# Left-over tokens of two batches interleaved in their buffer, and the last four stores walked token by token

## The chip, the cores and the metric

The kernel runs on one core of one Trainium2 chip. The metric is the device time of one execution in microseconds (us). The core has five engines that work side by side, each in its own program order: TensorE (PE, matrix products; PEld is its weight load), VectorE (DVE), ScalarE (ACT), GpSimd (POOL) and SyncE (SP). In this kernel SP issues every transfer; the transfers themselves are carried out by 16 DMA engines, between device memory and the on-chip buffers.

## The reference

The reference is an attention with keys and values averaged over blocks of 8 tokens, and two feed-forward blocks behind it:

```python
# q, k, v: 8 batches, 8 heads, 576 tokens, 64 per head
k_p = k.reshape(B, H, Sp, 8, D).mean(axis=3)
v_p = v.reshape(B, H, Sp, 8, D).mean(axis=3)
attn = softmax(q @ k_p^T / sqrt(D))
x = (attn @ v_p), heads side by side          # 4608 tokens x 512
h = x @ w_in                                   # 512 -> 1024
solu = h * softmax(h)
x = layernorm(solu) * g_ln @ w_out             # 1024 -> 512
h = ((x @ w1) * (x @ w2)) @ w3                 # 1024 -> 1024
out = h @ w_out2                               # 1024 -> 512, 4608 rows
```

All of it is in 32-bit floating point. Row 576 b + s of the output belongs to token s of batch b.

## The kernel before

**Tiles.** The 4608 tokens are nine blocks of 512. Blocks 0 to 7 are the first 512 tokens of the eight batches. Each batch has 64 tokens left over (`TL = S - 512`), and the eight left-overs together are block 8 (`j == B`). Up to the end of the first feed-forward block the unit of work is 256 tokens (`U`): 18 units, two to a block.

**First part.** Attention and the first feed-forward block run as one program in time slots (`put`, `after`). The instructions of every engine stand in the order in which the slots give them out. For each batch `Group.av` multiplies the softmax weights with the values. The result lies transposed, with 128 features on the partitions and tokens along the row, one call for each of the `NP = 4` feature chunks `p`. Of a batch's second group 256 tokens go on at once (`split`, an ACT copy at L100 and a DVE subtraction at L101), and the 64 left-over tokens are copied by DVE at L564 into the buffer `X8`. There are two such tiles, `X8[0]` for batches 0 to 3 and `X8[1]` for batches 4 to 7, 128 x (4 chunks x 256 tokens). Those copies number 8 batches x 4 chunks = 32. When units 16 and 17 come, `Rows.split_x` reads one `X8` tile each as a whole, and `Rows.chunk` takes its 256 tokens in two runs of 128.

So a token keeps its column of `X8` through everything behind it. Columns 128 i to 128 i + 127 of `X8[h]` become the 128 partitions of the output tile t = 2 h + i of block 8, and those 128 tokens come from batches 2 t and 2 t + 1.

**Second part.** Behind a stretch that prepares weights, the second feed-forward block runs block by block, `j` from 0 to 8, with all five engines in program order. `ab` makes the products (lines 948 to 950), `out_fc` adds them up in four accumulators `acc` (lines 994 to 997), and behind the last of eight steps `finish` ends the accumulators one after the other. `evac` scales each into an `ot` tile, 128 x 512, on DVE for even t (L1003) and on ACT for odd t (L1005), and SP issues its store (L1010). The four stores of a block are 256 KB each. For blocks 0 to 7, one row of 512 numbers per partition goes to a row of the output of its own. For block 8 the output rows lie in two batches, 576 rows apart.

The program ends when SP, at L1083, has seen every transfer land and the engines have met one another there.

Of the kernel before, what the change touches and what calls it, by code (L numbers as in the profile page):

```python
# [18 lines left out]
def attention_moe_kernel(  # L19
# [25 lines left out]
    nc = tc.nc  # L45

    B, H, S, D = q.shape
# [9 lines left out]
    TL = S - 512  # L57
    NB = B + 1
    NU = 2 * NB
    U = 256  # L60
# [12 lines left out]
    def bank(name):  # L73
        return PS.tile([P, 512], F32, tag="ba", name=name, bufs=3)
# [24 lines left out]
    def split(hi, lo, src):  # L99
        nc.scalar.activation(hi, src, AF.Copy)  # L100
        nc.vector.tensor_tensor(lo, src, hi.bitcast(F32), ALU.subtract)  # L101
# [43 lines left out]
    X8 = [X8P.tile([P, NP, U], F32, tag=f"X8{i}", name=f"X8{i}") for i in range(2)]  # L145
# [265 lines left out]
    class Group:  # L411
# [125 lines left out]
        def av(self, i):  # L537
            w, bt = self.width, self.batch
            if i == 0:
                X[self.a] = [M.tile([P, NP, U], F32R, tag=t, name=f"{t}{self.a}") for t in ("xh", "xl")]  # L540
            x = X[self.a]
            for p in (2 * i, 2 * i + 1):
                if self.g or p % 2 == 0:
                    av_bank = bank(f"av{self.a}_{p}")
                av = av_bank if self.g else av_bank[:, p % 2 * U : p % 2 * U + U]
                pair = lambda t: t[:, 2 * p : 2 * p + 2].rearrange("p a d -> p (a d)")
                vhp = VBDh[:, p].rearrange("p a d -> p (a d)")
                vlp = VBDl[:, p].rearrange("p a d -> p (a d)")
                terms = [
                    (vhp, self.pth[:, p, 0:w]),  # L550
                    (vhp, self.ptl[:, p, 0:w]),
                    (vlp, self.pth[:, p, 0:w]),
                    (pair(bt.vlh), self.ptx[:, 0:w]),
                    (pair(VLL), self.ptx[:, 0:w]),
                ]
                for n, (l, r) in enumerate(terms):
                    nc.tensor.matmul(av[:, 0:w], l, r, start=(n == 0), stop=(n == 4))  # L557
                if self.g == 0 and p % 2:
                    ps = slice(p - 1, p + 1)
                    split(x[0][:, ps], x[1][:, ps], av_bank.rearrange("p (c n) -> p c n", c=2))  # L560
                elif self.g == 1:
                    split(x[0][:, p], x[1][:, p], av[:, 0:U])
                    c0 = TL * (bt.b % 4)
                    nc.vector.tensor_copy(X8[bt.b // 4][:, p, c0 : c0 + TL], av[:, U : U + TL])  # L564


    class Rows:
# [216 lines left out]
    with tc.manual_schedule(engines={mybir.EngineType.PE, mybir.EngineType.SP}):  # L784
        for s_ in range(min(events), SLOTS * (NU + 1) + 2):
# [3 lines left out]
            u, c = s_ // SLOTS, s_ % SLOTS  # L789
# [209 lines left out]
    def evac(j, t):  # L999
        ot = M2.tile([P, C], F32, tag="ot", name=f"ot{j}_{t}", bufs=4)  # L1000
        k = kap[:, 4 * j + t : 4 * j + t + 1]
        if t % 2 == 0:
            nc.vector.tensor_scalar(ot, accs[t], k, None, ALU.mult)  # L1003
        else:
            nc.scalar.activation(ot, accs[t], AF.Copy, scale=k)  # L1005
        if j == B:
            to = out.rearrange("(b s) c -> b s c", s=S)[2 * t : 2 * t + 2, 512:S, :]
        else:
            to = out[S * j : S * j + 512, :].rearrange("(p t) c -> p t c", t=4)[:, t]
        nc.sync.dma_start(to, ot)  # L1010
# [3 lines left out]
    def finish():  # L1014

        nonlocal accs
        j, fc, pp = pend
        if fc == 0:
            accs = [bank(f"acc{j}_{t}") for t in range(4)]
        if fc < FC - 1:  # L1020
            for t in range(4):
                out_fc(fc, pp, t, False)
            for t in range(4):
                out_fc(fc, pp, t, True)
        else:
            for t in range(4):
                out_fc(fc, pp, t, False)
                out_fc(fc, pp, t, True)
                evac(j, t)
# [58 lines left out]
```

## Time and profile before

| | |
|---|---|
| median of three runs | 1296.38 us (1295.6 to 1296.57) |
| span of the profiled execution, first to last instruction | 1294.6 us |
| median less that span | 1.78 us |
| PE busy, share of the span | 1233.1 us, 95% |
| DVE busy | 807.7 us, 62% |
| ACT busy | 524.4 us, 41% |
| POOL busy | 406.1 us, 31% |
| granted TensorE clock, mean | 0.987 |
| stores of the output | 36, of 256 KB each |

The profile gives a span for the execution that it recorded and no total time of its own; the last 1.78 us of the median are what lies around the span, and they are carried along unchanged below. "Busy" counts the time in which an engine executes instructions; a share is an average over the whole span and says nothing of a stretch in which only one thing is left to wait for.

### The profile page before, as it was taken

To read this page: it belongs to the slowest core of one execution; us is meant where nothing else is said; L and a number is where in the kernel's file an instruction comes from. 1 tells how busy PE (TensorE), PEld (TensorE's weight loads), DVE (VectorE), ACT (ScalarE), POOL (GpSimd) and SP (SyncE) were. 2 spreads that over 40 slices of the span, in tenths; PEclk is the share of its full clock that TensorE was granted. 3 is DMA by queue.
4 is the path that set the end of the run, shared out by engine and by line. 5 is a ranking of instruction groups with operands and counts; after the bars stand their busy time and mean duration, and the time that the engine had idled before them with its cause. 6 is when DMAs were issued, how large, how long until landed. Compare 5 with 4: busy or idle time off the path is not lost.

```text
span 1294.6 us, 21828 instructions
## 1 busy us (share of the span) xinstructions
PE 1233.1 (95%) x8278; PEld 1126.2 (87%) x8278; DVE 807.7 (62%) x1595; ACT 524.4 (41%) x1480; POOL 406.1 (31%) x497
## 2 busy tenths in 40 slices
PE   7879999999999999999999999999999999999992
PEld 5669889888999888998987999999999999999991
DVE  6878777787878787635476454645454545454541
ACT  5554656666666666644354121212121212121210
POOL 3332534343534352300000243333333342424210
PEclk9989999999999999999999999999999999999996
DMA  9554556453646463223142011101010101010100
GB/s 232 123 131 126 143 128 166 116 162 110 174 117 171 116 163 110 74 74 114 41 170 83 1 33 34 58 10 66 1 66 1 66 1 66 1 66 1 34 1 33
DMA packets 85698, 109.43 MB, mean 85 GB/s; under 512 B 43608, under 2 KB 43608, under 8 KB 85592
## 3 DMA queue, kind: packets, MB, share of 16 engines
q1 hardware_dynamic: 85592, 108.03, 29.3%
q8 instruction: 65, 1.06, 0.3%
q14 instruction: 41, 0.34, 0.1%
HBM read 78.65 MB, written 29.36 MB: 83 GB/s over the span
## 4 chain that ended last, share of the span: by engine, by line
PE 73%; DVE 10%; DMA 7%; ACT 4%; issue 3%; POOL 1%; SPq 1%; POOLq 0%; DVEq 0%; ACTq 0%
PE p L948 9%; PE p L950 9%; PE p L949 9%; PE h L588 8%; PE acc L994 5%; PE acc L997 5%; PE acc L996 5%; PE x L646 3%; PE x L647 3%; PE x L645 3%; DMA f<-in_moe_w_dram 3%; PE av L557 2%; DMA kv<-in_v_dram 2%; PE lt L631 2%; DVE cvb L180 2%
## 5 line engine op out<-in xcount | busy, mean ns | idle before, releaser
L968 POOL TENSOR_TENSOR a<-a,b 128x256 f32<-128x256 f32 x72 | 53.0, 736 | 477.3 <-DVE b L967 477.3
L952 ACT ACTIVATE p<-p 128x256 f32<-128x256 f32 x72 | 27.9, 387 | 397.3 <-PE p L950 365.3
L645 PE MATMUL x<-lnh,gwh 128*128 128x256 f32 x576 | 166.4, 289 | 0.0
L646 PE MATMUL x<-lnl,gwh 128*128 128x256 f32 x576 | 163.0, 283 | 1.7 <-DVE lnl L635 1.7
L647 PE MATMUL x<-lnh,gwl 128*128 128x256 f32 x576 | 162.8, 283 | 0.0
L189 POOL TENSOR_TENSOR cvb<-cvb,cvm 128x512 f32<-128x512 f32 x46 | 61.0, 1326 | 187.3 <-DVE cvm L182 181.6
L473 ACT ACTIVATE ea<-sc,mx 128x72 f32<-128x72 f32 x320 | 98.6, 333 | 39.6 <-DVE mx L470 39.6
L997 PE MATMUL acc<-wfl,ph 128*128 128x512 f32 x288 | 113.1, 393 | 0.0
L996 PE MATMUL acc<-wfh,ph 128*128 128x512 f32 x288 | 112.9, 392 | 0.0
L646 PEld LDWEIGHTS x<-lnl,gwh 128*128 128x128 f32 x576 | 110.1, 191 | 2.8 <-DVE lnl L635 1.9
L645 PEld LDWEIGHTS x<-lnh,gwh 128*128 128x128 f32 x576 | 109.9, 191 | 1.0 <-DVE lnl L635 0.2
L647 PEld LDWEIGHTS x<-lnh,gwl 128*128 128x128 f32 x576 | 110.0, 191 | 0.0
L967 DVE TENSOR_TENSOR b<-b,p 128x256 f32<-128x256 f32 x72 | 30.2, 420 | 123.0 <-PE p L950 123.0
L588 PE MATMUL h<-winh,xh 128*128 128x512 f32 x288 | 98.8, 424 | 0.0
L588 PE MATMUL h<-winl,xh 128*128 128x512 f32 x288 | 90.0, 394 | 0.0
L588 PE MATMUL h<-winh,xl 128*128 128x512 f32 x288 | 89.4, 392 | 0.0
L948 PE MATMUL p<-th,w1h 128*128 128x256 f32 x288 | 81.6, 283 | 1.1 <-ACT p L952 1.1
L994 PE MATMUL acc<-wfh,pl 128*128 128x512 f32 x288 | 82.4, 392 | 0.0
L949 PE MATMUL p<-th,w1h 128*128 128x256 f32 x288 | 81.5, 283 | 0.0
L950 PE MATMUL p<-th,w1l 128*128 128x256 f32 x288 | 81.5, 283 | 0.0
L635 DVE TENSOR_TENSOR lnl<-lt,lnh 128x512 fp32r<-128x512 f32 x72 | 49.2, 686 | 51.2 <-ACT lnh L634 50.8
L956 DVE TENSOR_TENSOR u<-p,p 128x256 f32<-128x256 f32 x72 | 30.4, 422 | 77.3 <-PE p L950 76.2
(201 smaller groups left out, 3728.1 us busy)
## 6 DMA issues: line engine op xcount, KB each, us to landing
f<-in_moe_w_dram SPq DMA_DIRECT2D x32, 512.0 KB, 6.0
x2d<-xo SPq DMA_DIRECT2D x36, 256.0 KB, 2.0
xq<-x2d SPq DMA_DIRECT2D x36, 256.0 KB, 2.8
out_dram<-ot SPq DMA_DIRECT2D x36, 256.0 KB, 2.7
kv<-in_k_dram SPq DMA_DIRECT2D x32, 256.0 KB, 3.7
q<-in_q_dram SPq DMA_DIRECT2D x32, 256.0 KB, 7.5
kv<-in_v_dram SPq DMA_DIRECT2D x32, 256.0 KB, 6.7
f<-in_moe_w_out_dram SPq DMA_DIRECT2D x16, 512.0 KB, 6.2
```

Of the source, the lines that this page charges most:

```text
L189: self.engine.tensor_tensor(self.f, self.f, self.m.bitcast(F32), ALU.add)
L473: nc.scalar.activation(e[0:n, x], half[a][:, h], AF.Exp, bias=mx[0:n, x : x + 1], scale=1.0, accum_out=sm[0:n, x : x + 1],)
L588: nc.tensor.matmul(self.ph[:, a], s_[:, c], w_[:, c, a * 512 : a * 512 + 512], start=first, stop=last)
L645: nc.tensor.matmul(o, gw[0][:, f, ws], self.th[:, f], start=(f == 0), stop=False)
L646: nc.tensor.matmul(o, gw[0][:, f, ws], self.tl[:, f], start=False, stop=False)
L647: nc.tensor.matmul(o, gw[1][:, f, ws], self.th[:, f], start=False, stop=(f == FC - 1))
L948: nc.tensor.matmul(o, wh[:, c, fsl], th[:, c], start=c == 0, stop=False)
L949: nc.tensor.matmul(o, wh[:, c, fsl], tl[:, c], start=False, stop=False)
L950: nc.tensor.matmul(o, wl[:, c, fsl], th[:, c], start=False, stop=c == 1)
L994: nc.tensor.matmul(accs[t], pl[:, ts], wh, start=False, stop=(fc == FC - 1))
L996: nc.tensor.matmul(accs[t], ph[:, ts], wh, start=(fc == 0), stop=False)
L997: nc.tensor.matmul(accs[t], ph[:, ts], wl, start=False, stop=False)
```

## The change

Two places are edited. The copy at L564 writes the 64 left-over tokens of a batch to every second column of a run of 128 columns, so that column 2 s + b holds token s of batch b of the pair, where before the two batches' tokens lay in two runs of 64. The view of the output at the last four stores follows: it names the 64 tokens first and the two batches second.

```diff
@@ -560,8 +560,8 @@
                 elif self.g == 1:
                     split(x[0][:, p], x[1][:, p], av[:, 0:U])
-                    c0 = TL * (bt.b % 4)
-                    nc.vector.tensor_copy(X8[bt.b // 4][:, p, c0 : c0 + TL], av[:, U : U + TL])
+                    left = X8[bt.b // 4][:, p].rearrange("p (g s b) -> p g b s", g=2, b=2)[:, bt.b % 4 // 2, bt.b % 2]
+                    nc.vector.tensor_copy(left, av[:, U : U + TL])
@@ -1004,7 +1004,7 @@
         if j == B:
-            to = out.rearrange("(b s) c -> b s c", s=S)[2 * t : 2 * t + 2, 512:S, :]
+            to = out.rearrange("(b s) c -> s b c", s=S)[512:S, 2 * t : 2 * t + 2, :]
         else:
             to = out[S * j : S * j + 512, :].rearrange("(p t) c -> p t c", t=4)[:, t]
         nc.sync.dma_start(to, ot)
```

The instructions of PE, DVE, ACT and POOL stand in the same order as before. On SP the last four stores differ, at the very end of its program; `ot_0` to `ot_3` are the four output tiles, and behind each stands the shape of the output's view, outermost first:

```order
 L1010 DMA out_dram<-ot_2_13222 128x512
 L1010 DMA out_dram<-ot_3_13228 128x512
-L1010 DMA out_dram<-ot_0_13790 2x64x512
-L1010 DMA out_dram<-ot_1_13796 2x64x512
-L1010 DMA out_dram<-ot_2_13802 2x64x512
-L1010 DMA out_dram<-ot_3_13808 2x64x512
+L1010 DMA out_dram<-ot_0_13790 64x2x512
+L1010 DMA out_dram<-ot_1_13796 64x2x512
+L1010 DMA out_dram<-ot_2_13802 64x2x512
+L1010 DMA out_dram<-ot_3_13808 64x2x512
 L1083 UNCONDITIONAL_BRANCH
```

Nothing has moved; the two outer sizes of the four stores have changed places. The two lines above them are stores of block 7, whose view is 128 rows.

## Rows read from the trace of the kernel before

**Rows 1.** The profile's page: span, busy time, and DMA packets by size.

```profile
span 1294.6 us, 21828 instructions
PE 1233.1 (95%) x8278; PEld 1126.2 (87%) x8278; DVE 807.7 (62%) x1595; ACT 524.4 (41%) x1480; POOL 406.1 (31%) x497
...
DMA packets 85698, 109.43 MB, mean 85 GB/s; under 512 B 43608, under 2 KB 43608, under 8 KB 85592
```

**Rows 2.** Busy time by stretch at the end; last columns clock, DMA share, GB/s.

```profile
1269.40:1270.50 1.10, 1.10 (x6) 0.69 (x4) 0.51 (x1) 0.60 (x1) 0.00 (x0) 1.00 0.03 7
1270.50:1274.00 3.50, 0.13 (x1) 0.00 (x0) 0.24 (x1) 0.69 (x1) 0.00 (x0) 1.00 0.12 26
1274.00:1293.00 19.00, 0.00 (x0) 0.00 (x0) 0.00 (x0) 0.00 (x0) 0.00 (x0) 0.52 0.13 50
1293.00:1293.50 0.50, 0.00 (x0) 0.00 (x0) 0.00 (x0) 0.00 (x0) 0.00 (x0) 0.50 0.03 12
1293.50:1294.60 1.10, 0.00 (x0) 0.00 (x0) 0.00 (x0) 0.00 (x0) 0.00 (x0) 0.50 0.00 0
```

**Rows 3.** Timeline of block 8's evictions and stores: start, us, engine, line.

```profile
1268.63 0.75 DVE L1003 TENSOR_SCALAR ot<-acc,kap 128x512 f32<-128x512 f32 x1 [0.75 <-PE acc L994]
...
1269.31 0.69 ACT L1005 ACTIVATE ot<-acc,kap 128x512 f32<-128x512 f32 x1 [2.15 <-PE acc L994]
...
1269.41 10.67 SPq L1010 DMA_DIRECT2D out_dram<-ot  x4
...
1270.67 0.69 ACT L1005 ACTIVATE ot<-acc,kap 128x512 f32<-128x512 f32 x1 [0.67 <-PE acc L994]
```

**Rows 4.** L1010, block 8's four stores: issue ns min/median/max, first and last start.

```profile
L1010 SPq DMA_DIRECT2D out_dram<-ot x4: 559/2390/5035, 1269.4 to 1275.0; - x4
```

**Rows 5.** Who waited for whom on SP, from 1265 us to the end.

```profile
SPq L1083 <- DMA out_dram<-ot: 13.5, 2, 8.4
SPq L1083 <- PEq L1083: 0.6, 2, 0.4
```

**Rows 6.** L1010, block 7's four stores, with time to landing.

```profile
L1010 SPq DMA_DIRECT2D out_dram<-ot x4: 332/335/338, 1209.9 to 1211.8; - x4
...
DMA to landing us min/median/max: 2.8/2.8/2.8
```

**Rows 7.** Timeline: block 7's last eviction.

```profile
1211.07 0.69 ACT L1005 ACTIVATE ot<-acc,kap 128x512 f32<-128x512 f32 x1 [0.68 <-PE acc L994]
```

**Rows 8.** Busy time by stretch around block 7's stores; last columns as in rows 2.

```profile
1208.00:1210.50 2.50, 2.50 (x12) 1.79 (x11) 1.94 (x5) 0.69 (x1) 0.00 (x0) 1.00 0.00 0
1210.50:1214.00 3.50, 3.50 (x30) 3.42 (x29) 1.49 (x3) 1.26 (x3) 1.43 (x2) 1.00 0.89 300
1214.00:1216.00 2.00, 2.00 (x19) 2.00 (x18) 1.46 (x4) 0.45 (x1) 0.00 (x0) 1.00 0.00 0
```

**Rows 9.** L300, the loads of keys (views 64 x 2 x 512): issue ns min/median/max.

```profile
L300 SPq DMA_DIRECT2D kv<-in_k_dram x32: 597/604/780, 1.3 to 453.4; - x32
```

**Rows 10.** Timeline of SP at the program's start, with two such loads.

```profile
0.74 0.45 SPq L95 DMA_DIRECT2D gT<-in_moe_g_ln_dram  x1
1.25 1.40 SPq L300 DMA_DIRECT2D kv<-in_k_dram  x2
2.69 0.72 SPq L308 DMA_DIRECT2D KL<-in_k_dram  x1
3.46 0.39 SPq L157 DMA_DIRECT2D f<-in_moe_w_in_dram  x1
```

**Rows 11.** Busy time by stretch there; last columns as in rows 2.

```profile
2.80:3.20 0.40, 0.00 (x0) 0.00 (x0) 0.03 (x1) 0.00 (x0) 0.40 (x2) 1.00 0.62 159
3.20:3.60 0.40, 0.00 (x0) 0.00 (x0) 0.40 (x2) 0.00 (x0) 0.40 (x2) 1.00 0.76 282
3.60:4.00 0.40, 0.00 (x0) 0.00 (x0) 0.30 (x3) 0.00 (x0) 0.40 (x2) 1.00 1.04 292
```

**Rows 12.** L1083, the program's end: SP's closing instructions from 1290 us on.

```profile
L1083 SPq EVENT_SEMAPHORE  x6: 17/28/28, 1293.6 to 1294.6; - x6
```

**Rows 13.** L564, the copies into X8, and who waited for them (us, times).

```profile
L564 DVE COPY X<-av x32: 212/215/217, 81.4 to 561.5; 128x64 f32<-128x64 f32 x32
...
  PE pt L518: 5.7, 6
  PE av L557: 0.4, 1
  PEld sc L452: 0.2, 1
```

**Rows 14.** Three other lines of DVE: ns min/median/max, starts, shapes.

```profile
L180 DVE SCALAR_TENSOR_TENSOR cvb<-f,cvb x56: 640/692/1670, 12.3 to 544.1; 128x512 int32<-128x512 int32 x56
L529 DVE TENSOR_TENSOR ptl<-pt,pth x40: 417/681/693, 32.9 to 549.4; 128x512 fp32r<-128x512 f32 x32, 128x256 fp32r<-128x256 f32 x8
L406 DVE TENSOR_TENSOR sl<-vl,sh x8: 220/1001/1059, 31.9 to 469.9; 64x64 f32<-64x64 f32 x8
```

## The prediction

> **What bounds the kernel now.** The page gives a span of 1294.6 us with PE busy for 95% of it [rows 1]. That share says that PE sets the time while there is work for PE. It does not say what sets the end, so I read the last stretch by itself, as a table of busy time. From 1274 us to the end no engine computes anything: PE, DVE, ACT and POOL are all at zero, and all that moves is data at 50 GB/s [rows 2]. The timeline gives the start of this tail. Block 8's four accumulators are scaled out one after the other; the last of these evictions, on ACT, starts at 1270.67 us and takes 0.69 us, so it ends at 1271.36 [rows 3]. From there to the end of the span are 1294.6 - 1271.36 = 23.2 us with nothing but the four output stores. The view of waits agrees: SP's closing wait is for these stores, 13.5 us in two waits, and there is no other of size [rows 5].
>
> Why is the tail long? The four stores hold 4 x 256 KB = 1.05 MB. Between 1274 and 1293 us the mean busy share of the 16 DMA engines is 0.13 [rows 2], and 0.13 x 16 = 2.1: two engines, at 50 / 2 = 25 GB/s each, carry everything. 1.05 MB at 50 GB/s is 21 us, which is the tail but for its ends. Two is also the outermost size of the store's view of the output, two batches.
>
> **The same stores elsewhere in this trace.** Block 7 ends in the same way: two DVE and two ACT evictions, four stores of 256 KB, but the view's outermost size is 128. Its last eviction starts at 1211.07 and ends at 1211.76 us [rows 7]. Data flows from 1210.5 to 1214.0 us at a DMA share of 0.89 and 300 GB/s, and the share is 0.00 behind 1214.0 [rows 8]; 3.5 us x 300 GB/s is again 1.05 MB. So these data stop at latest 1214.0 - 1211.76 = 2.24 us behind the last eviction. SP issues each store in 0.34 us [rows 6]; in block 8 an issue takes between 0.56 and 5.04 us [rows 4].
>
> **The change part by part.** *The stores.* The outermost size becomes 64. No store of this kind is in the trace, but loads of the keys have just these views, 64 x 2 x 512 on both sides, 256 KB each. Their issue takes 0.60 us [rows 9]. At the program's start two of them are issued at 1.25 us, ahead of a load of 128 KB at 2.69 us [rows 10], and from 3.2 to 4.0 us the DMA share is 0.76 to 1.04 at 282 to 292 GB/s [rows 11]. So an outermost size of 64 brings close to all 16 engines, and an issue costs 0.60 - 0.34 = 0.26 us more than block 7's.
>
> The Trainium skill (DMA: Bandwidth & Descriptors, section "Why a DMA increments its semaphore by 16 and not by 1") has a rule for this: a transfer runs on the largest number of engines, up to 16, that divides the outermost size of both its sides. By it 2 gives two engines, with which the share of 0.13 agrees, and 64 against the tile's 128 partitions gives 16; a store with 64 outermost is what no run here shows yet. It would leave the sum as it is and speaks against the narrow rivals below.
>
> The new tail is then, from the last eviction's end: 2.24 us until the data stop, as behind block 7; 0.26 us for the longer issue; and the program's own end. Of that end, the old tail shows the size: some data still move between 1293.0 and 1293.5 us, 12 GB/s x 0.5 us = 6 KB, which at 50 GB/s is 0.12 to some 0.3 us of flow as one or both engines finish, so the data stop near 1293.3, and 1.3 us later the span ends [rows 2]. Sum 2.24 + 0.26 + 1.3 = 3.8 us, against 23.2 us. The span becomes 1271.4 + 3.8 = 1275.2 us, 19.4 us less. The landing time of block 7's stores gives nearly the same by another way: 2.8 us from issue to landing [rows 6], 0.26 for the longer issue and the 1.0 us from SP's first closing instruction behind the data, at 1293.6 us, to the end [rows 12] make 4.1.
>
> Bounds for this term: without the longer issue, and with block 7's data stopping up to 0.3 us before its stretch's edge, 3.2 us. If the stores run at the lower rate of the loads, 282 for 300 GB/s, and both the issue's 0.26 us and a first piece of data late by as much again come on top, 2.24 + 0.25 + 0.52 + 1.3 = 4.3 us. What hides the longer issue is the step between evictions: 1269.31 to 1270.67 is two steps, 0.68 us each [rows 3], just over an issue of 0.60 us. Little queues up behind it on SP, and only the closing wait stands there.
>
> *The copies into X8.* 32 copies of 128 x 64 go on, 212 to 217 ns each [rows 13], now with every second word of the target skipped. None writes like that in this trace. The nearest row is L180, which reads every second word of one operand over 512 columns: median 692 ns. L529 with neighbouring words takes 681 ns for most of its calls of that width [rows 14]. So a step of two costs nothing that shows. The upper bound is a copy that pays for twice the columns. L529 takes 417 ns at its shortest, the 256-column form, and 681 at 512: 264 / 256 = 1.03 ns per column, hence 64 x 1.03 = 66 ns per copy and 32 x 66 ns = 2.1 us if every one lay on the path. PE and its weight load waited for a copy only 6 + 1 + 1 = 8 times in 32 [rows 13]; so counted it is 0.5 us. DVE is 62% busy [rows 1], which covers the rest. I take 0, and keep 0 to 2.1 us.
>
> The Trainium skill (SBUF — State Buffer, section "Door 1: The DMA port swizzle") says that a step of up to four 32-bit words, that is two accesses or more in a line of 16 bytes, runs at full rate. That is the zero end, where the sum already stands; the rows of reads agree, and no row here shows it for writes.
>
> *What stays.* The two batches' tokens sit in other columns, but the reader of X8 takes the whole tile, the products run over the same columns, and the order of instructions on PE, DVE, ACT and POOL is the same. Up to 1271.4 us I expect no difference.
>
> **The time.** 1294.6 - 19.4 = 1275.2 us of span. The median of the runs is 1.78 us over the profiled span, and I carry that over: **1277.0 us**, 1.5% less.
>
> **The rivals.** *Some engines only (0.02 for four, 0.02 for eight).* The spread could follow the inner size or a fixed part of 64. With 4 engines, 1.05 MB / (4 x 25 GB/s) = 10.5 us. Block 8's data begin about 1270.7, in the stretch of 25 to 26 GB/s [rows 2], so they stop at 1281.2, the span ends at 1282.5 and the time is 1284.3. With 8 engines, 5.2 us, it would be 1279.0, inside the range. The loads' share of 0.76 to 1.04 speaks against both.
>
> *SP's issue is the cost (0.03).* The last two of the four issues share 10.67 us with the first two [rows 3], and one takes 5.04 us [rows 4]. If that is the price of writing in pieces to two batches, not of waiting for two busy engines, the fourth still ends at 1269.41 + 10.67 = 1280.1 us. Its data then need about 1 us more, and the end 1.3 us: 1282.4, a time of 1284.2. Against it: the shortest of the four takes 0.56 us with the same form, so the length comes from what is queued in front; and key loads of the same form take 0.60 us at the median [rows 9].
>
> *No change (0.03).* The two inner rows of a token could be cut out as the outer loop again, or the partitions decide, and two engines carry all: 1296.4 us, as before.
>
> *Slower (0.01).* The mechanism would be the strided copies. L406, a smaller DVE instruction, 64 x 64, takes 1001 ns at the median and 220 at best [rows 14], so a short DVE instruction can be stretched by something beside it. If each copy took 1.0 us, 32 x 0.785 = 25 us, and PE waited for all of it, the time would be 1277.0 + 25 = 1302 us. It decides from 19.4 / 32 = 0.61 us more per copy on the path. L180's reads and the 8 waits in 32 speak against it.
>
> **How the numbers follow.** The forecast has 0.89. Its own spread: 0.6 us less for the short tail and 0.8 us for a run like the fastest of before (1295.6 against 1296.38) at the low end, which is 1275.6; at the high end 0.5 us of tail and 2.1 us of copies, 1279.6. I give 1275.5 to 1279.8. The rivals outside it hold 0.02 + 0.03 + 0.03 + 0.01 = 0.09, so it need not reach to them. A measurement tells about 0.2%, 2.6 us, from no change. Faster than that: the forecast, the partly spread stores and the issue, 0.89 + 0.04 + 0.03 = 0.96. Within: 0.03. Slower: 0.01.
>
> **What would show it.** In the profile after: from 1270.5 to 1274 us a DMA share near 0.9 and about 300 GB/s, where 0.12 and 26 stood; four issues at L1010 of 0.6 us each, none of several us; nothing left behind about 1275.3 us; SP's closing wait for the stores at some 2 us; L564 still near 215 ns. The prediction is wrong if the share stays at 0.13 or stops at a quarter or half, if the issues stay long, or if the last eviction ends later than 1271.4 us by more than 1 us, which would point to the copies.

## The result and the profile after

The changed kernel takes 1275.57 us in the median of four runs (1274.38 to 1277.2), against 1296.47 us of the kernel before on the same chip. The ratio is 0.9843, with a 95% interval of 0.9829 to 0.9857. The prediction was 1277.0 us, in a range of 1275.5 to 1279.8 us. The profiled execution took 1277.2 us, with a span of 1275.4 us, where the prediction's sum gave 1275.2.

The page of the changed kernel, to be held against [rows 1]: span, busy time, packets.

```profile
span 1275.4 us, 21828 instructions
PE 1230.8 (97%) x8278; PEld 1124.8 (88%) x8278; DVE 807.3 (63%) x1595; ACT 525.1 (41%) x1480; POOL 406.6 (32%) x497
...
DMA packets 85754, 109.43 MB, mean 86 GB/s; under 512 B 43664, under 2 KB 43664, under 8 KB 85648
```

The same instructions move the same bytes. There are 56 more packets under 512 B, and 14 more engines in each of four stores make 56: each engine that takes part in a store adds one small packet of its own, and the other outermost sizes below bear that out. The busy time by stretch at the end, columns as in [rows 2], shows the rest:

```profile
1269.40:1270.50 1.10, 1.10 (x6) 0.67 (x4) 0.53 (x1) 0.58 (x1) 0.00 (x0) 1.00 0.02 7
1270.50:1274.00 3.50, 0.11 (x1) 0.00 (x0) 0.22 (x1) 0.69 (x1) 0.00 (x0) 1.00 0.79 302
1274.00:1274.50 0.50, 0.00 (x0) 0.00 (x0) 0.00 (x0) 0.00 (x0) 0.00 (x0) 1.00 0.00 0
1274.50:1275.40 0.90, 0.00 (x0) 0.00 (x0) 0.00 (x0) 0.00 (x0) 0.00 (x0) 0.80 0.00 0
```

Up to the last eviction this is the kernel before. Then 302 GB/s flow where 26 to 50 did, for 3.5 us in place of some 22, and nothing is left behind 1274 us. The timeline of the last eviction and of the stores, the issues at L1010 and the copies at L564 (ns, min/median/max), and SP's closing wait (us, times, longest):

```profile
1269.39 2.59 SPq L1010 DMA_DIRECT2D out_dram<-ot  x4
...
1270.65 0.69 ACT L1005 ACTIVATE ot<-acc,kap 128x512 f32<-128x512 f32 x1 [0.67 <-PE acc L994]
```

```profile
L1010 SPq DMA_DIRECT2D out_dram<-ot x4: 561/562/630, 1269.4 to 1271.4; - x4
...
L564 DVE COPY X<-av x32: 210/215/217, 81.2 to 561.2; 128x64 f32<-128x64 f32 x32
...
SPq L1083 <- DMA out_dram<-ot: 2.4, 2, 1.4
```

The last eviction ends at 1270.65 + 0.69 = 1271.34 us, 0.02 us from where it ended before [rows 3]. The four issues take 2.59 us together, not 10.67, and none is long [rows 3, 4]. The closing wait fell from 13.5 to 2.4 us [rows 5], and a copy takes the same 215 ns [rows 13]. From the last eviction's end to the end of the span, called the tail below, are 1275.4 - 1271.34 = 4.1 us, where 23.2 were.

### The profile page after: what moved, and what is told of

It is laid out like the page before. It is cut to its first block, busy times and chain, and to the rows that moved or that the text cites. A ratio compares the mean times of both kernels' runs of the same rounds, so it can differ in the third digit from the quotient of the medians.

```text
span 1275.4 us, 21828 instructions
## 1 busy us (share of the span) xinstructions
PE 1230.8 (97%) x8278; PEld 1124.8 (88%) x8278; DVE 807.3 (63%) x1595; ACT 525.1 (41%) x1480; POOL 406.6 (32%) x497
## 2 busy tenths in 40 slices
DMA packets 85754, 109.43 MB, mean 86 GB/s; under 512 B 43664, under 2 KB 43664, under 8 KB 85648
## 4 chain that ended last, share of the span: by engine, by line
PE 77%; DVE 9%; DMA 5%; ACT 5%; issue 2%; SPq 1%; POOL 0%; DVEq 0%; ACTq 0%; POOLq 0%
PE h L588 11%; PE p L948 9%; PE p L950 9%; PE p L949 9%; PE acc L994 5%; PE acc L997 5%; PE acc L996 5%; PE x L646 3%; PE x L647 3%; PE x L645 3%; DMA f<-in_moe_w_dram 3%; PE av L557 2%; PE lt L631 2%; ACT ea L473 2%; PE sc L452 1%
```

## The experiments

Where a view's outermost size is changed alone, the rows of block 8 land in another order or place than the reference's, as each expectation says; the times read as those of a kernel that moves the same bytes. The four kernels named outer_ ran once each; they are read by their profiles, not by their times.

**The stores alone, and the copies alone.** Each takes one hunk of the change.

```diff
# stores_alone: the kernel before, with
-            to = out.rearrange("(b s) c -> b s c", s=S)[2 * t : 2 * t + 2, 512:S, :]
+            to = out.rearrange("(b s) c -> s b c", s=S)[512:S, 2 * t : 2 * t + 2, :]
# copies_alone: the kernel before, with
-                    nc.vector.tensor_copy(X8[bt.b // 4][:, p, c0 : c0 + TL], av[:, U : U + TL])
+                    left = X8[bt.b // 4][:, p].rearrange("p (g s b) -> p g b s", g=2, b=2)[:, bt.b % 4 // 2, bt.b % 2]
+                    nc.vector.tensor_copy(left, av[:, U : U + TL])
```

> Only the view of the last four stores is changed; the copies into X8 write as before, so the 512 rows of block 8 land in another order than the reference's. Theory (the gain is the spread of the last stores over the DMA engines, the copies cost nothing): all of the gain, a span near 1275.4 us, 4.1 us from the last eviction's end to the end of the span, ratio to before 0.984. Rival (strided copies give or take something in the first part): the time differs from that of the full change by up to 2 us, and the last eviction ends at another time than 1271.3 us.

> Only the copies into X8 are changed; the last four stores keep the two batches outermost, so the rows of block 8 land in another order than the reference's. Theory: no change, ratio 1.000 within 0.002, L564 at 215 ns per copy, 23.3 us from the last eviction's end to the end of the span. Rival (a strided write is dearer): L564 at up to 281 ns and up to 2.1 us more.

The stores alone gave 1279.75 us, ratio 0.9862 (0.9839 to 0.9885). The copies alone gave 1297.61 us, ratio 1.0009 (0.9990 to 1.0029). Each kernel's profile, first the stores alone (span, the last eviction, the four issues):

```profile
span 1278.9 us, 21828 instructions
...
1274.10 0.69 ACT L1005 ACTIVATE ot<-acc,kap 128x512 f32<-128x512 f32 x1 [0.67 <-PE acc L994]
...
L1010 SPq DMA_DIRECT2D out_dram<-ot x4: 560/571/636, 1272.8 to 1274.9; - x4
```

and the copies alone:

```profile
span 1292.4 us, 21828 instructions
...
1268.38 0.69 ACT L1005 ACTIVATE ot<-acc,kap 128x512 f32<-128x512 f32 x1 [0.67 <-PE acc L994]
...
L1010 SPq DMA_DIRECT2D out_dram<-ot x4: 552/2412/5036, 1267.1 to 1272.8; - x4
L564 DVE COPY X<-av x32: 212/215/218, 80.6 to 560.1; 128x64 f32<-128x64 f32 x32
```

The tail goes with the stores: 1278.9 - 1274.79 = 4.1 us with the new view, 1292.4 - 1269.07 = 23.3 us with the old one. A strided copy takes 215 ns, so no price per copy shows. But the last eviction ends at 1274.8 us in one and at 1269.1 us in the other, where 1271.4 was expected. That is taken up below.

**How the outermost size acts.** The view of the last four stores is cut three other ways, with the copies as before.

```diff
# outer_4, outer_8, outer_16: the kernel before, with one of
+            to = out.rearrange("(b s) c -> b s c", s=S)[t // 2 * 4 :, 512 + t % 2 * 32 :, :][:4, :32]
+            to = out.rearrange("(b s) c -> b s c", s=S)[:, 512 + 16 * t : 528 + 16 * t, :]
+            to = out.rearrange("(b s) c -> s b c", s=S)[512 + 16 * t : 528 + 16 * t, :, :]
```

> The last four stores walk 4 batches outermost and 32 tokens inside, with the copies as before, so the rows of block 8 land in another order. Theory (the outermost size sets how many DMA engines carry a store): four engines, a DMA share of 0.25 and about 102 GB/s behind the last eviction, 1.05 MB in 10.3 us from 1270.7, span 1282.3 us, time 1284.1 us; some issues on SP still several us long. Rival (any size but two spreads over all engines): span near 1275.4 us. Rival (long issues come from the form of the view): issues as long as with two outermost.

> The last four stores walk 8 batches outermost and 16 tokens inside, with the copies as before, so the rows of block 8 land in another order. Theory: eight engines, a DMA share of 0.5 and about 204 GB/s, 1.05 MB in 5.1 us from 1270.7, span 1277.2 us, time 1279.0 us, tail of 5.9 us behind the last eviction. Rival (any size but two spreads over all engines): span near 1275.4 us, tail 4.1 us.

> The last four stores walk 16 tokens outermost and 8 batches inside, with the copies as before, so the rows of block 8 land in another order. Theory (the outermost size sets the number of DMA engines, and 16 is all of them): the tail behind the last eviction is that of 64 outermost, 4.1 us, at a DMA share near 0.8 and 300 GB/s, with issues of 0.56 to 0.65 us. Rival (the outermost size must be larger, or rows that alternate over eight batches are dearer): a tail of 5 to 8 us as with 8 outermost, where it was 8.2 us.

For each, the last eviction, the four issues, and the busy time from about that eviction on, with DMA share and GB/s last; for four and eight, narrower stretches stand under it. Four outermost (span 1287.6 us, time 1289.39):

```profile
1273.48 0.69 ACT L1005 ACTIVATE ot<-acc,kap 128x512 f32<-128x512 f32 x1 [0.67 <-PE acc L994]
...
L1010 SPq DMA_DIRECT2D out_dram<-ot x4: 557/606/1782, 1272.2 to 1274.3; - x4
...
1274.00:1286.00 12.00, 0.00 (x0) 0.00 (x0) 0.00 (x0) 0.17 (x1) 0.00 (x0) 0.66 0.24 86
1273.50:1276.00 2.50, 0.00 (x0) 0.00 (x0) 0.05 (x1) 0.67 (x1) 0.00 (x0) 1.00 0.24 32
1276.00:1285.00 9.00, 0.00 (x0) 0.00 (x0) 0.00 (x0) 0.00 (x0) 0.00 (x0) 0.60 0.26 101
```

Eight outermost (span 1279.8 us, time 1281.58):

```profile
1270.89 0.69 ACT L1005 ACTIVATE ot<-acc,kap 128x512 f32<-128x512 f32 x1 [0.67 <-PE acc L994]
...
L1010 SPq DMA_DIRECT2D out_dram<-ot x4: 604/654/1014, 1269.6 to 1271.8; - x4
...
1271.50:1278.00 6.50, 0.00 (x0) 0.00 (x0) 0.00 (x0) 0.08 (x1) 0.00 (x0) 0.72 0.47 155
1272.50:1274.50 2.00, 0.00 (x0) 0.00 (x0) 0.00 (x0) 0.00 (x0) 0.00 (x0) 0.97 0.53 196
```

Sixteen outermost (span 1277.5 us, time 1279.24):

```profile
1272.06 0.69 ACT L1005 ACTIVATE ot<-acc,kap 128x512 f32<-128x512 f32 x1 [0.67 <-PE acc L994]
...
L1010 SPq DMA_DIRECT2D out_dram<-ot x4: 561/564/617, 1270.8 to 1272.8; - x4
...
1272.00:1276.00 4.00, 0.02 (x1) 0.00 (x0) 0.13 (x1) 0.69 (x1) 0.00 (x0) 0.92 0.83 264
```

The DMA share follows the outermost size: 0.13, 0.24, 0.47 and 0.83 for 2, 4, 8 and 16 are 2.1, 3.8, 7.5 and 13.3 engines of 16, with idle ends in the last. The packets count the engines without that blur: 85706, 85722 and 85754 with 4, 8 and 16 outermost are 8, 24 and 56 more than before, which is 2, 6 and 14 more engines in each of four stores. So it is the outermost size that sets the number of engines, up to all 16, for the sizes run here, which are powers of two; the prediction's rivals in which the inner size or the partitions decide are out. The rule of the Trainium skill that the prediction cites (DMA: Bandwidth & Descriptors, section "Why a DMA increments its semaphore by 16 and not by 1") held in all five cases, 2, 4, 8, 16 and 64.

The tails with 4, 8 and 16 outermost are 13.4, 8.2 and 4.75 us. Sixteen lies between its theory (4.1) and its rival (5 to 8), with all 16 engines at work. With four and eight the tails are longer than expected (10.9 and 5.9). The means of 86 and 155 GB/s suggest engines that are slower throughout, but they hold the ends of the stretch as well. In the middle four engines carry 101 GB/s and eight carry 196, some 25 GB/s each, as two do (50 / 2). What four lose lies at the start, 32 GB/s for 2.5 us while a share of 0.24 says that all four are busy, and at the end, where 42 GB/s flow at a share of 0.11 from 1285.0 to 1286.5 us, as if the four did not finish together. Eight lose time in the same two ways, with 78 GB/s at 0.46 from 1271.0 to 1272.5 us and 83 at 0.22 from 1277.0 to 1278.5, and in a dip to 147 GB/s from 1274.5 to 1276.0.

Long issues shrink with the number of engines, 5.0, 1.8 and 1.0 us at most, then none, while the shortest issue of two and of four is 0.56 us, in views of the same form. That fits a wait behind stores whose engines are still busy, and not a price of the view.

**The distance between the rows.** One more kernel asked whether the eight runs' distance in the output slows eight engines.

```diff
# outer_8_near: the kernel before, with
+            r0 = 2 * S * t + 430
+            to = out[r0 : r0 + 136].rearrange("(o i) c -> o i c", i=17)[:, 0:16]
```

> As outer_8, eight runs of 16 rows outermost, but the eight runs lie 17 rows (34 KB) apart in the output instead of 576 rows (1152 KB); they go to rows of block 0, 2, 4 and 6, and the rows of block 8 are not written. With outer_8 the tail was 8.2 us where eight engines at 24 GB/s each, the rate of two, would give 6.1. Theory (the wide distance between the runs that eight engines write at the same time is what slows them): a tail of 6.1 us and some 195 GB/s. Rival (eight engines on 16 partitions each are slower by themselves, wherever they write): a tail near 8.2 us and 140 GB/s again.

The same three rows of this kernel (span 1276.4 us):

```profile
1267.60 0.69 ACT L1005 ACTIVATE ot<-acc,kap 128x512 f32<-128x512 f32 x1 [0.67 <-PE acc L994]
...
L1011 SPq DMA_DIRECT2D out_dram<-ot x4: 604/652/1048, 1266.3 to 1268.5; - x4
...
1268.20:1274.70 6.50, 0.00 (x0) 0.00 (x0) 0.00 (x0) 0.08 (x1) 0.00 (x0) 0.68 0.46 155
```

155 GB/s again, and a tail of 1276.4 - 1268.29 = 8.1 us. The theory of the distance fell: eight engines take as long with the runs 34 KB apart as with 1152 KB. The rows are not all those that the expectation names: the last three of a store's eight runs, and two rows of the one ahead of them, fall on left-over rows of a batch, which belong to block 8. The distance, which is what the kernel varies, is as stated.

**Without interleaving.** If only the engines per store count, the buffer can stay as it was and each tile can go out in two stores.

```diff
# two_stores: the kernel before, with
+            for h in range(2):
+                r0 = S * (2 * t + h) + 512
+                nc.sync.dma_start(out[r0 : r0 + TL, :], ot[TL * h : TL * h + TL])
# two_stores_two_queues: the same, with
+                (nc.scalar if h else nc.sync).dma_start(out[r0 : r0 + TL, :], ot[TL * h : TL * h + TL])
```

> No interleaving: the copies as before, and each of the last four tiles goes out in two stores of 64 x 512, one per batch, eight stores in all; the output is the reference's. Theory (only the number of engines per store counts): the same gain, ratio 0.984; issues of 0.34 us as for block 7, and a tail of 3.6 to 4.1 us behind the last eviction, since two issues take 0.7 us where one took 0.56, but the last one starts its data sooner and holds half of them. Rival (half tiles spread over fewer engines, or cost more each): a tail above 5 us.

> As two_stores, but the second batch's stores are issued by ACT, the first batch's by SP; the output is the reference's. Theory (what is left of the tail is issue, data and the program's end): the last issue starts 0.4 us sooner, a tail of 3.2 to 3.7 us, ratio 0.984, no difference that a measurement of the whole can tell. Rival (an issue on ACT holds up its next eviction): the last eviction ends 0.3 us or more later behind the first, and the gain is lost.

Medians 1279.6 us (0.9868, 0.9846 to 0.9889) and 1279.43 us (0.9869, 0.9846 to 0.9892). The issues of the first, and its last eviction (span 1281.6 us):

```profile
L1009 SPq DMA_DIRECT2D out_dram<-ot x8: 546/570/593, 1273.8 to 1278.3; - x8
...
1275.09 0.69 ACT L1005 ACTIVATE ot<-acc,kap 128x512 f32<-128x512 f32 x1 [0.67 <-PE acc L994]
```

An issue takes 0.57 us, not 0.34, though the view has no inner pair. Two issues per tile, 1.2 us, are slower than the 0.68 us between evictions; SP falls behind, issues the last store 2.5 us behind the last eviction's end, and the tail is 5.8 us. The rival was right: half tiles cost more. But their issue is not all that they cost. The profile has 85818 packets, 120 more than before, which is 16 engines in each of the eight stores. The busy time of a stretch behind the eviction's start, first of this kernel, then of the changed one:

```profile
1275.00:1280.00 5.00, 0.05 (x1) 0.00 (x0) 0.16 (x1) 0.69 (x1) 0.00 (x0) 0.84 0.88 206
```

```profile
1271.00:1273.00 2.00, 0.00 (x0) 0.00 (x0) 0.00 (x0) 0.34 (x1) 0.00 (x0) 1.00 1.04 400
```

The engines are busy for 0.88 of the time and move 206 GB/s, where with whole tiles a share of 1.04 moves 400. If they only waited for SP, they would stand idle between the halves. So a busy engine moves a half tile at some 60% of the rate; which of the two, this rate or the issue, sets the 5.8 us, these runs do not separate. The timeline of ACT in the second kernel (span 1274.9 us):

```profile
1267.81 0.58 ACTq L1009 DMA_DIRECT2D out_dram<-ot  x1
1268.49 0.69 ACT L1005 ACTIVATE ot<-acc,kap 128x512 f32<-128x512 f32 x1 [2.94 <-PE acc L994]
1269.21 1.42 ACTq L1009 DMA_DIRECT2D out_dram<-ot  x2
1270.73 0.69 ACT L1005 ACTIVATE ot<-acc,kap 128x512 f32<-128x512 f32 x1 [1.55 <-issue]
```

Its tail is 3.5 us, as the theory said. But ACT's issues stand ahead of its own evictions: the last one waits 1.55 us on "issue" and ends 4.4 us behind the first eviction's start at 1267.02, where the changed kernel needs 2.7. The rival was right too: the tail gains 0.6 us, and 1.7 are lost ahead of it.

**A last tile in two queues.** Only the last tile is split, where ACT has no eviction left to hold up.

```diff
# last_two_queues: the changed kernel, with
+        if (j, t) == (B, 3):
+            nc.scalar.dma_start(to[32:64], ot[64:P])
+            to, ot = to[0:32], ot[0:64]
         nc.sync.dma_start(to, ot)
```

> The changed kernel, but the very last tile goes out in two halves of 32 tokens x 2 batches, one issued by SP and one by ACT, whose own eviction it is; the output is the reference's. Theory (ACT has nothing left to do behind its last eviction, so its issue holds up nothing): evictions as in the changed kernel, 2.7 us from the first's start to the last's end, and a tail of 3.5 us where the changed kernel has 4.1; the whole differs from the changed kernel's by 0.6 us, less than its measurement tells. Rival (two halves cost more than one store): a tail of 4.1 us or more.

Median 1277.3 us, ratio 0.986 (0.9844 to 0.9875). The last eviction starts at 1270.91 us and the span is 1275.5 us, a tail of 3.9 us: a third of the expected 0.6 us, and nothing that the whole can show. The engines again move little while they are busy, near the end of the data:

```profile
1273.00:1273.50 0.50, 0.00 (x0) 0.00 (x0) 0.00 (x0) 0.00 (x0) 0.00 (x0) 1.00 0.96 213
```

None of the three splits beat the changed kernel.

**Do the copies cost, or bring, anything?** One kernel doubles the copy, two repeat the full change and the stores alone on one chip.

```diff
# copies_twice: the changed kernel, with
                     nc.vector.tensor_copy(left, av[:, U : U + TL])
+                    nc.vector.tensor_copy(left, av[:, U : U + TL])
```

> The changed kernel with each of the 32 copies into X8 done twice, 6.9 us more work for DVE; the output is the same. Theory (the copies lie mostly beside other work, and PE waited for 8 of 32): 0.2 us each on 8 of them, up to 1.7 us more, median 1275.6 to 1277.3, ratio to before 0.984 to 0.985. Rival (the copies are on the path): 6.9 us more, median 1282.5, ratio 0.989. The tail behind the last eviction stays at 4.1 us in both.

> The changed kernel once more, on one chip with the stores alone, since the two gave medians 4.2 us apart on different chips (1275.57 and 1279.75 us), with the same tail of 4.1 us. Theory (the first part ends some us sooner or later from run to run, whatever the kernel, and the copies cost and bring nothing): the medians of the two agree within 2 us, ratio to before 0.985 for both. Rival (the strided copies shorten the first part by some 2 us or more): this one is faster by 3 to 4 us again.

> Only the view of the last four stores is changed, as in stores_alone (rows of block 8 land in another order). Theory: within 2 us of after_again's median, ratio 0.985. Rival (the strided copies bring 3 to 4 us): slower than after_again by 3 to 4 us, ratio 0.988.

The doubled copies gave 1274.32 us, ratio 0.9823 (0.9799 to 0.9847), a median below both forecasts: no time lost that shows for 6.9 us of added work, and the rival's 0.989 lies outside the interval. The copies lie beside other work.

The full change again gave 1276.64 us, ratio 0.9857 (0.9837 to 0.9876), and the stores alone 1279.82 us, ratio 0.9868 (0.9847 to 0.9889). The medians are 3.2 us apart. The theory, 2 us at most, missed, and this is the distance that the rival named; but the ratios differ by 0.0011, with intervals that overlap widely. With the earlier runs each kernel has nine executions: their mean spans are 1274.7 and 1277.6 us, 2.9 us apart with a standard error of 1.0 (though not all on one chip), while single ones go from 1272.6 to 1278.5 and from 1272.8 to 1280.0. The profiles show where the distance lies. L655 stores the first part's results; the row's last time is the start of the last such store, and the row under it the last eviction. In order: before, the full change (its first profile), the copies alone, the stores alone again, and the earliest and the latest of all, with eight outermost nearby and with two stores.

```profile
L655 SPq DMA_DIRECT2D x2d<-xo x36: 319/326/334, 116.7 to 654.4; - x36
```

```profile
L655 SPq DMA_DIRECT2D x2d<-xo x36: 319/326/333, 116.7 to 654.6; - x36
```

```profile
L655 SPq DMA_DIRECT2D x2d<-xo x36: 319/326/334, 115.3 to 652.2; - x36
```

```profile
L655 SPq DMA_DIRECT2D x2d<-xo x36: 319/326/333, 120.1 to 658.0; - x36
...
1274.19 0.69 ACT L1005 ACTIVATE ot<-acc,kap 128x512 f32<-128x512 f32 x1 [0.67 <-PE acc L994]
```

```profile
L655 SPq DMA_DIRECT2D x2d<-xo x36: 319/326/333, 116.2 to 651.4; - x36
```

```profile
L655 SPq DMA_DIRECT2D x2d<-xo x36: 319/326/333, 117.1 to 658.8; - x36
```

From the last store of the first part to the start of the last eviction are 616.3, 616.1, 616.2 and 616.2 us in the first four: the second part takes the same time, and the 5.8 us between the kernels arise ahead of 658 us. The first such store already stands 4.8 us apart (115.3 and 120.1 us). That the first part scatters by itself is seen in the nine profiles with the copies of before: the first part is the same program in all of them, and its last store starts anywhere from 651.4 to 658.8 us. The five with strided copies lie inside, from 652.2 to 654.7. With the new stores the strided copies go with less time (1276.6 against 1279.8 us), with the old ones with a little more (ratio 1.0009). So no cost of the copies shows; whether they save up to some 3 us in the first part stays open, and so does the source of the scatter.

## Why the prediction was right

**What bounds the end.** Right. The last stores were a stretch with no other work, and two engines carried them. The outer sizes from 4 to 16 show the number of engines as a series.

**The stores' term.** The predicted tail was 3.8 us (bounds 3.2 to 4.3); it is 4.1 us in each profile of the new view. The issue was put at 0.60 us and takes 0.56. The data were to stop 2.24 + 0.26 = 2.5 us behind the last eviction, by 1273.9 us; the table of stretches has them stop by 1274.0, and what follows to the end of the span takes about 1.4 us, 1.3 forecast. That 302 GB/s met the 300 of the forecast says little, since both are the same 1.05 MB over stretches of 3.5 us. In the middle the new stores move 400 GB/s, and the share over the stretch was 0.79 where 0.9 was forecast. The prediction took the longer issue from loads with an inner pair in the view. The pair is not what makes it long: a store of 64 plain rows takes 0.57 us, and the shortest with 2, 4 or 16 outermost 0.56, where block 7's, with 128 rows outermost, take 0.34.

**The copies' term.** Zero cost was right as far as the runs tell: 215 ns per copy before and after, and doubling them cost nothing measurable. The upper bound of 2.1 us was not needed. That the copies might bring time was not considered, and the 2.9 us between the full change and the stores alone leave it open.

**The time.** The span of the profiled execution, 1275.4 us, is 0.2 us from the sum. That it came so close is in part luck: the last eviction of this execution ended within 0.02 us of its place in the kernel before, while in the second profile of the same kernel it ended at 1270.8 us. The median, 1275.57 us, is 1.4 us below the forecast because the other three runs had spans of 1272.6 to 1274.6 us, and it lies only 0.07 us inside the range. The prediction allowed 0.8 us for the spread of runs; the first part scatters by several, and which side of the lower bound the median fell on was chance. The fall of some 19 us in the stores' stretch doesn't hang on it.

**The rivals.** Some engines only: out, the share is 0.79. Issue on SP as the cost: out; long issues went away with the free engines. No change: out. Slower by the copies: out. The price put on four and eight engines in that rival, 25 GB/s each, holds in the middle of the stretch but not for the whole of it: measured, four take a tail of 13.4 us where its sum has 11.1 (1282.5 - 1271.4), since they start slowly and move little at the end.

## What to carry to other kernels

Read the end of a kernel as a stretch of its own: a mean of 95% busy hid 23 us in which two of 16 DMA engines worked. A DMA share that stands still at a small fraction, times 16, names the number of engines, and the outermost size of a transfer's view is the first thing to compare it with. Where the natural order puts a small size outermost, change the order in which the rows lie on the partitions upstream, where it is free; splitting the transfer instead costs an issue each, 0.57 us here, against 0.68 us between tiles, and the halves moved 206 GB/s where whole tiles moved 400. Before a rate per engine is taken from a stretch, look at the stretch in parts: its ends can hide in the mean.

## What was not expected of the hardware

Busy engines did not always move data at the same rate. In the middle of a stretch two, four, eight and 16 of them moved some 25 GB/s each (50, 101, 196 and, with 64 outermost, 400 GB/s). But two moved only 26 GB/s together at a share of 0.12 over the first 3.5 us [rows 2], and four 32 GB/s at 0.24 over the first 2.5 us, while with 64 outermost the first half microsecond, 1270.5 to 1271.0, has 250 GB/s at 0.63, the full rate for its share. And half tiles moved 206 GB/s at 0.88. The spacing of the rows in memory had no part in the rate at eight (155 GB/s at 34 KB and at 1152 KB). What slows busy engines there, no run here shows. Sixteen outermost with eight rows inside was 0.7 us longer in the tail than 64 with two, at the same issue times; from 1274.0 to 1275.5 us it moved 261 GB/s, and why stays open.
